# First layer's last four token blocks in two pairs by seven products, and another order of the seven

## The chip, the core and the metric

One core of one Trainium2 chip runs the whole program. The time is device microseconds of one execution; the kernel before takes 1685.62 us (median of three runs, 1683.19 to 1685.78). The engines are named as in the profile: PE (TensorE, matmuls), PEld (its weight loads), DVE (VectorE), ACT (ScalarE), POOL (GpSimd), SP (SyncE, which issues the DMAs).

## What is computed

Linear attention with a normalization, then two layers of a two-matrix network on 4608 tokens of 512 values, the hidden width being 2048:

```python
kv = einsum('bhsd,bhse->bhde', k, v);  out = einsum('bhsd,bhde->bhse', q, kv)   # 8 batches, 8 heads, 576 tokens, 64
x = out / sqrt(mean(out * out, -1) + 1e-06) * g_norm                            # -> [4608, 512]
r = maximum(x @ w_in1, 0);   x = (s * (r * r) + b) @ w_out1                     # first layer
h = x @ w_in2;               y = (h * (1 / (1 + exp(-h)))) @ w_out2             # second layer
```

The weights come as 64-bit floats.

## The kernel before, in words

**Tiles.** Tokens go in nine blocks of 512 (`NB = 9`): block t < 8 holds 512 of batch t's 576 tokens, block 8 the 64 that are left of each. A block of activations is four tiles of 128 x 512. Every fp32 operand of a matmul is split into a rounded part `hi` (written by ACT) and a rest `lo` (a subtraction with two SBUF inputs on DVE or POOL, line 191), and each product takes three matmuls: hi x hi, hi x lo, lo x hi.

**A unit** (`unit`, L611 on) is one block with one 128-wide slice m of the hidden width, m = 0..15: 12 matmuls into a bank `h` (`mm1`), the activation, square and affine on ACT and DVE, the split into `gh` and `gl`, and 12 matmuls that add into four banks `acc` (`mm2`), which come 1.6 units later. The first layer is nine blocks of 16 units. During a block, `attention_pair` (L368 on) makes the next block's activations, two heads at a time, in four steps; `decode` (L219 on) turns the 64-bit weights into fp32; `factors` (L320 on) does so for the second layer's weights, forms the four sums that the seven products want and writes eight quarters of each weight in split form to DRAM.

**Pairs.** In the second layer blocks 0 to 7 go in four pairs by Strassen's seven products, for the hidden product alone. `pair_x` (L760 on) loads half the inner dimension of two blocks (kk = 0 or 1) into the one tile `x32`, forms T1 to T4 (four subtractions of 128 x 512, three of them in the tile `xt`) and splits seven operands into the tiles `xo0..xo6`. `hidden(tp, j)` (L820 on) does two slices of the hidden width at once: seven products of six matmuls in three banks X, Y, Z, in the order X, Y, Z, X, Y, Y, Z. Between two products that share a bank DVE reads the bank (x1, u2, u3, h22): these are partial sums, and the next product adds on top. `outputs(tp, j)` (L919 on) multiplies by the second matrix as before: eight tiles of six matmuls, each added by DVE into a sum `y2` in SBUF (L940). One j is thus 42 + 48 matmuls in place of 48 + 48. The last block goes by units.

**Order.** All instructions are handed to `Plan`, which sorts them by a key (units of the program) and by costs of its own for every engine, and emits each engine's list in a fixed order. At run time each engine goes through its list in that order and waits at whatever is not ready. SBUF space changes hands by name: `lent_to` says which weight tile becomes which `xo`, `win`, `wout` or `g2` tile once the first layer's last block has used it:

```python
        wanted = [f"xo{i}{kk}" for i in range(7) for kk in range(KH)] + ["win"] * 6 + ["wout"] * 5 + ["g2"] * 7
                lent_to[f"w{kind}{m}"] = wanted[2 * m + (kind == "o")]
```

## Time and profile before

| | |
|---|---|
| median of 3 runs | 1685.62 us (1683.19 to 1685.78) |
| the profiled execution | 1683.55 us, its span 1681.2 us |
| PE busy | 1642.5 us (98%), 7744 matmuls |
| DVE, ACT, POOL busy | 51%, 39%, 34% |
| chain that ended last | PE 91% |
| mean granted TensorE clock | 0.991 |

How to read it: busy times are shares of an engine's own time and say nothing of who waits. Matmuls overlap in the records (one lasts some 390 ns, but the next begins long before it ends), so the rate of PE is read from how many start in a stretch, or from the chain of waits, not from the mean of one. A stretch of the windows view gives busy time and instructions of each engine, the granted clock, the share of the DMA engines and GB/s. In time the program is: 0 to 80 us start and block 0, blocks 1 to 8 by units up to 906 us, four pairs up to 1575 us, the last block up to 1662 us, the last store.

### The profile page before, as it was taken

The page shows a single profiled execution, that of the slowest core. Times are in us where ns is not written, and L with a number is a line of the kernel's source. Part 1 is how long each engine was busy: PE and PEld are TensorE (multiplying, and loading weights), DVE is VectorE, ACT ScalarE, POOL GpSimd, SP SyncE. Part 2 cuts the span into 40 slices and gives each one's busy share as a digit, 9 for nine tenths or more (in the row PEclk, how much of TensorE's full clock was granted, in tenths as well). Part 3 has the DMA queues.
Part 4 walks back from the last instruction along what each step waited for, and adds up shares of the span by engine and source line. Part 5 has one row for each costly group of instructions (what it writes and reads, how often), then busy time and mean ns, then how long its engine had stood idle before and what let it go on. Part 6 is the DMA issues. An engine that isn't in the chain of part 4 may idle for free.

```text
span 1681.2 us, 21306 instructions
## 1 busy us (share of the span) xinstructions
PE 1642.5 (98%) x7744; PEld 1334.1 (79%) x7744; DVE 865.4 (51%) x1313; ACT 658.5 (39%) x1198; POOL 565.3 (34%) x481
## 2 busy tenths in 40 slices
PE   8889999999999999999999999999999999999995
PEld 6667888888888888888887888888888888888884
DVE  6998666675656666534342244634463445344211
ACT  5666444444444444432333322432343234323221
POOL 4665343333434344210341223622362235223100
PEclk9989999999999999999999999999999999999998
DMA  9554445444444544210134444644464447444552
GB/s 218 173 157 125 134 127 158 139 147 126 138 143 129 168 122 150 99 63 1 51 116 128 126 145 140 229 156 143 142 232 148 139 138 237 138 140 141 183 156 81
DMA packets 226911, 236.28 MB, mean 141 GB/s; under 512 B 99832, under 2 KB 181752, under 8 KB 226680
## 3 DMA queue, kind: packets, MB, share of 16 engines
q1 hardware_dynamic: 226680, 234.94, 45.4%
q8 instruction: 61, 1.00, 0.3%
q14 instruction: 42, 0.34, 0.1%
q0 software_dynamic: 128, 0.00, 0.0%
HBM read 181.41 MB, written 53.48 MB: 140 GB/s over the span
## 4 chain that ended last, share of the span: by engine, by line
PE 91%; DVE 3%; DMA 1%; ACT 1%; issue 1%; SPq 1%; POOL 0%; DVEq 0%; ACTq 0%; POOLq 0%
PE hp L836 18%; PE h L184 8%; PE h L185 8%; PE h L183 8%; PE acc L183 8%; PE acc L184 7%; PE acc L185 7%; PE acc L931 7%; PE acc L932 7%; PE acc L930 7%; PE kv_ps L433 1%; PE acc L687 1%; PE acc L686 1%; PE acc L685 1%; DVE raw L263 1%
## 5 line engine op out<-in xcount | busy, mean ns | idle before, releaser
L836 PE MATMUL hp<-xo,win 128*128 128x512 f32 x1344 | 344.0, 390 | 0.8 <-DVE tmp L861 0.8
L191 POOL TENSOR_TENSOR g<-tmp,g 128x512 fp32r<-128x512 f32 x123 | 159.3, 1296 | 425.0 <-ACT g L188 223.5
L836 PEld LDWEIGHTS hp<-xo,win 128*128 128x128 f32 x1344 | 252.0, 188 | 57.6 <-DVE tmp L861 2.2
L940 DVE TENSOR_TENSOR y<-acc,y 128x512 f32<-128x512 f32 x224 | 154.3, 690 | 275.1 <-PE acc L932 273.0
L183 PE MATMUL acc<-gh,wo 128*128 128x512 f32 x576 | 234.4, 407 | 2.9 <-ACT gh L188 2.9
L184 PE MATMUL acc<-gl,wo 128*128 128x512 f32 x576 | 226.9, 394 | 5.8 <-DVE gl L191 2.8
L629 ACT ACTIVATE g<-h 128x512 f32<-128x512 f32 x160 | 95.5, 597 | 346.8 <-PE h L185 337.6
L184 PE MATMUL h<-xl,wi 128*128 128x512 f32 x576 | 226.8, 394 | 1.7 <-DVE xl L191 1.6
L183 PE MATMUL h<-xh,wi 128*128 128x512 f32 x576 | 226.5, 393 | 0.1
L185 PE MATMUL h<-xh,wi 128*128 128x512 f32 x576 | 226.1, 393 | 0.3 <-DVE wi L191 0.3
L185 PE MATMUL acc<-gh,wo 128*128 128x512 f32 x576 | 226.1, 392 | 0.0
L637 DVE SCALAR_TENSOR_TENSOR g<-g,vecs 128x512 f32<-128x512 f32 x128 | 104.0, 813 | 197.1 <-ACT g L629 197.0
L932 PE MATMUL acc<-wout,g 128*128 128x512 f32 x512 | 201.7, 394 | 0.0
L931 PE MATMUL acc<-wout,g 128*128 128x512 f32 x512 | 201.7, 394 | 0.0
L930 PE MATMUL acc<-wout,g 128*128 128x512 f32 x512 | 201.3, 393 | 0.0
L861 DVE TENSOR_TENSOR tmp<-hp,tmp 128x512 f32<-128x512 f32 x160 | 110.4, 691 | 99.3 <-PE hp L836 93.9
L665 DVE SCALAR_TENSOR_TENSOR gl<-g,vecs,gh 128x512 fp32r<-128x512 f32 x128 | 112.4, 878 | 49.3 <-ACT gh L659 48.1
L282 POOL TENSOR_TENSOR dw<-raw 128x256 uint32<-128x256 uint32 (+1 forms) x100 | 88.8, 890 | 137.3 <-DVE raw L268 87.3
L184 PEld LDWEIGHTS acc<-gl,wo 128*128 128x128 f32 x576 | 108.9, 189 | 28.1 <-DVE gl L191 4.4
L191 POOL TENSOR_TENSOR spill<-dw,spill 128x512 fp32r<-128x512 f32 x53 | 71.5, 1350 | 176.5 <-ACT spill L188 171.2
L184 PEld LDWEIGHTS h<-xl,wi 128*128 128x128 f32 x576 | 109.0, 189 | 27.2 <-DVE xl L191 3.7
L183 PEld LDWEIGHTS acc<-gh,wo 128*128 128x128 f32 x576 | 109.0, 189 | 26.4 <-ACT gh L188 4.2
(123 smaller groups left out, 2303.1 us busy)
## 6 DMA issues: line engine op xcount, KB each, us to landing
win<-wi SPq DMA_DIRECT2D x96, 512.0 KB, 4.5
wout<-wo SPq DMA_DIRECT2D x160, 256.0 KB, 4.1
wi<-spill SPq DMA_DIRECT2D x32, 512.0 KB, 2.6
wo<-spill SPq DMA_DIRECT2D x32, 512.0 KB, 2.9
win<-wi SPq DMA_DIRECT2D x64, 256.0 KB, 3.2
raw<-in_moe_w_out_dram SPq DMA_DIRECT2D x38, 256.0 KB, 3.0
y<-y SPq DMA_DIRECT2D x36, 256.0 KB, 2.6
raw<-in_moe_w_in_dram SPq DMA_DIRECT2D x34, 256.0 KB, 2.8
```

What stands on the lines that cost most here:

```text
L183: nc.tensor.matmul(ps, wh, xh, start=first, stop=False)
L184: nc.tensor.matmul(ps, wh, xl, start=False, stop=False)
L185: nc.tensor.matmul(ps, wl, xh, start=False, stop=last)
L191: eng[e].tensor_tensor(lo, src, f32(hi), op=ALU.subtract)
L637: nc.vector.scalar_tensor_tensor(out=g_t[u], in0=g_t[u], scalar=s_t, in1=g_t[u], op0=ALU.mult, op1=ALU.mult)
L665: nc.vector.scalar_tensor_tensor(out=st["g"][1], in0=g_t[u], scalar=b_t, in1=f32(st["g"][0]), op0=ALU.add, op1=ALU.subtract)
L836: nc.tensor.matmul(ps, w[:, wn, f_], x_[:, xn], start=first and n == 0, stop=kk == KH - 1 and n == 2, skip_group_check=True)
L861: nc.vector.tensor_tensor(t, bank[me, a], tmp[b_, me], op=ALU.add)
L930: nc.tensor.matmul(ps, g[:, 0, dd], w[:, 0], start=f == 0, stop=False)
L931: nc.tensor.matmul(ps, g[:, 0, dd], w[:, 1], start=False, stop=False)
L932: nc.tensor.matmul(ps, g[:, 1, dd], w[:, 0], start=False, stop=f == 1)
L940: nc.vector.tensor_tensor(y2[tp, tt], st["ps"], y2[tp, tt], op=ALU.add)
```

## The change

**First layer.** Five blocks (`NPL = 5`) go by units; blocks 5 and 6, and 7 and 8, go in two pairs by the same seven products as in the second layer; six pairs in all (`PAIRS`), the second layer's four behind them.

- The activations of blocks 5 to 8 are written to DRAM (`x1_d`) and loaded again by `pair_x`. Attention for blocks 2 to 6 is put into the first five blocks, more densely (a table of keys), for block 7 into the first pair, and block 8 (`last_block`) behind it.
- `factors_first` forms the four sums of the first layer's `w_in` for each j, splits them and writes them to DRAM, with the three plain quarters that are multiplied and all 16 tiles of `w_out`, since these tiles are lent out after block 4 and not after block 8. In each j: two additions of 128 x 512, four of 128 x 256, two roundings and two rests of 128 x 512 (ACT; DVE or POOL), and nine DMAs on SP.
- `xt` loses its place in the pool `l2p` and becomes tile `wi12`, lent after block 4's slice 12; `win` has 5 places in the first layer's pairs (6 before), and 7 later; the tiles `g`, `gh`, `gl` and `y` are handed on as `tmp`.
- In the first layer's pairs each of the four hidden tiles of a j takes a square and an affine step beside the activation (ACT, DVE or POOL); bank Y is one of the four `acc` banks, since attention has `at`.
- `factors` for the second layer's 16 sets is spread over keys 6.4 apart (6 before), and so runs into the first pair.

**Both layers.** The seven products are made in the order X, Y, Z, Y, X, Y, Z: the two products on Y that followed one another directly now have one on X between them. `T4` takes the place of B21 in `x32`.

The core of the diff:

```diff
@@ constants and buffers
-    NPR = (NB - 1) // 2
+    NPL = 5
+    PAIRS = [(0, t) for t in range(NPL, NB, 2)] + [(1, t) for t in range(0, NB - 1, 2)]
+    NPR = len(PAIRS)
...
-    A11, S2, S1, A12, S3, A22, S4, A21 = range(8)
+    A11, S2, S1, S3, A12, A22, S4, A21 = range(8)
@@ def factors_first(j, key), new
+        for f in range(2):
+            add(both(DM), key + 0.1 * f, total(f), needs=[("late",), ("mm1o", KF + 2 * j, 0)] + whole("i", 2 * j + f) + [("fw", 0) + me] * f,
+                makes=[("fw", f) + me], takes=[("dw2", me)] * (f == 0), gives=w_lent("i", 2 * j + f))
+        for o, a, b_, op in ((4, 2, 3, ALU.add), (6, 0, 2, ALU.subtract), (5, 4, 0, ALU.subtract), (7, 1, 5, ALU.subtract)):
...
+            add(both(QW), key + 0.3 + 0.02 * o, go, needs=[("fw", 1) + me] + ([("sum", o - 1 if o == 5 else 5) + me] if o in (5, 7) else []),
+                makes=[("sum", o) + me])
...
+            add(act(2 * QW), key + 0.7 + 0.1 * g, hi, needs=sums, makes=[("fh", g) + me], takes=[sp])
+            add(both(2 * QW), key + 0.72 + 0.1 * g, lo, needs=[("fh", g) + me], makes=[("fl", g) + me], gives=[("dw2", me)])
@@ normalize
+        if paired:
+            add({"SP": 0.48}, key + 0.9, lambda e: dma(x1_d[t, :, p], st["xa"]), needs=[("x32", t, p)], makes=[("xd", t, p)],
+                gives=[xb], move=0.73)
@@ units
-    units = {(l * NB + t) * KF + m: (l, t, m) for l in range(2) for t in range(NB) for m in range(KF) if l == 0 or t == NB - 1}
+    units = {(l * NB + t) * KF + m: (l, t, m) for l in range(2) for t in range(NB) for m in range(KF) if t == NB - 1 or t < NPL
+             if (t < NPL) == (l == 0)}
@@ pairs
-    B11, T2, T1, B21, T3, T4, B22 = range(7)
+    B11, T2, T1, T3, B21, T4, B22 = range(7)
-    BANK = (X, Y, Z, X, Y, Y, Z)
+    BANK = (X, Y, Z, Y, X, Y, Z)
@@ pair_x
-                dma(t[:, 2 * h:2 * h + 2], y1[2 * tp:2 * tp + 2, :, kk + KH * h].rearrange("n p t -> p n t"))
+                dma(t[:, 2 * h:2 * h + 2], (x1_d, y1)[layer][n0:n0 + 2, :, kk + KH * h].rearrange("n p t -> p n t"))
-                    st["t"] = pools["l2p"].tile([P, 3, T], F32, tag="xt", name="xt")
+                    st["t"] = f32(place(("xt", me)))
@@ hidden
+        ybank = "at" if layer else "acc"
-        read = {3: "x1", 4: "u2", 5: "u3", 6: "h22"}
+        read = {3: "u2", 4: "x1", 5: "u3", 6: "h22"}
...
+            if layer == 0:
+                add({**act(T), **both(T)}, kk + 0.03, squares, needs=[last], makes=[("sq2",) + q_])
+                add({**act(T), DVE: 0.46}, kk + 0.06, affine, needs=[("sq2",) + q_], makes=[("sa",) + q_])
@@ program
-                factors(kind, j, KF + 3 + 6 * (2 * j + n))
+                factors(kind, j, KF + 3 + 6.4 * (2 * j + n))
+            factors_first(j, 20 + 6 * j)
-        wanted = [f"xo{i}{kk}" for i in range(7) for kk in range(KH)] + ["win"] * 6 + ["wout"] * 5 + ["g2"] * 7
+        wanted = [f"xo{i}{kk}" for i in range(7) for kk in range(KH)] + ["win"] * 5 + ["wout"] * 5 + ["xt"] + ["g2"] * 7
+        more = {"tmp": 4, "g2": 3, "win": 2}
-                    attention_pair(t, p, KF * (t - 1) + (0.5 + 3.2 * p if t > 1 else 0.75 + 3.4 * p))
-                split_x(t, p, KF * t - 0.8)
+                    k0, dk = {1: (0.75, 3.4), 2: (16.5, 3), 3: (32.5, 2.8), 4: (48.5, 2.2), 5: (57, 2.2), 6: (65, 2.2), 7: (80, 3)}[t]
+                    attention_pair(t, p, k0 + dk * p)
+                if t < NPL:
+                    split_x(t, p, KF * t - 0.8)
-        last_block(KF * (NB - 2) + 6)
+        last_block(94)
```

**What moves in the engines' lists.** The lists of all engines are the same as before up to block 1's first unit (on PE the first 824 rows, on DVE the first 198; the program's lines have other numbers in the changed kernel: L183 to L185 are L186 to L188, L191 is L194, L836 is L922, L861 is L947, L940 is L1050). In the names, `_49` and the like in brackets are semaphores of the engine or DMA lane that is waited for.

First place: PE, where the units end and the first pair begins, from the first product's kk = 0 on. Before (block 8 to the second layer's first pair):

```order
L836 MATMUL hp_8240<-xo00_7693,win_7923 128x512 [waits DMAHW6_49]
L836 MATMUL hp_8240<-xo00_7693,win_7923 128x512 [waits Pool_49]
L836 MATMUL hp_8240<-xo00_7693,win_7923 128x512
L183 MATMUL acc_7712<-gh_8216,wo14_1662 128x512
L184 MATMUL acc_7712<-gl_8217,wo14_1662 128x512
L185 MATMUL acc_7712<-gh_8216,wo14_1662 128x512
L836 MATMUL hp_8240<-xo01_7956,win_7923 128x512
L836 MATMUL hp_8240<-xo01_7956,win_7923 128x512 [waits Pool_49]
L836 MATMUL hp_8240<-xo01_7956,win_7923 128x512
```

Now (block 4 to the first layer's first pair), and on to slice 15:

```order
L922 MATMUL hp_5595<-xo00_5415,win_5105 128x512 x2
L186 MATMUL acc_4704<-gh_5527,wo14_1687 128x512
L187 MATMUL acc_4704<-gh_5528,wo14_1687 128x512
L188 MATMUL acc_4704<-gh_5527,wo14_1687 128x512
L922 MATMUL hp_5595<-xo01_5549,win_5105 128x512 [waits Activation_49]
L922 MATMUL hp_5595<-xo01_5549,win_5105 128x512 [waits DVE_49]
L922 MATMUL hp_5595<-xo01_5549,win_5105 128x512
L186 MATMUL acc_4741<-gh_5527,wo14_1687 128x512
L187 MATMUL acc_4741<-gh_5528,wo14_1687 128x512
L188 MATMUL acc_4741<-gh_5527,wo14_1687 128x512
L186 MATMUL acc_4672<-gh_5601,wo15_1755 128x512 [waits Activation_49]
L187 MATMUL acc_4672<-gh_5602,wo15_1755 128x512 [waits DVE_49]
```

The same turn has moved from behind block 8 to behind block 4, with the same products between; `xo01`, the operand of kk = 1, now comes from DVE and not from POOL.

Second place: DVE at that same turn. Before, the rows ahead of the first read of bank Y (L861):

```order
L637 SCALAR_TENSOR_TENSOR g_8174<-g_8174,vecs_103 128x512 [waits Activation_49]
L665 SCALAR_TENSOR_TENSOR gl_8185<-g_8174,vecs_103,gh_8184 128x512 [waits PE_49,Activation_49]
L637 SCALAR_TENSOR_TENSOR g_8206<-g_8206,vecs_103 128x512 [waits Activation_49]
L665 SCALAR_TENSOR_TENSOR gl_8217<-g_8206,vecs_103,gh_8216 128x512 [waits PE_49,Activation_49]
L637 SCALAR_TENSOR_TENSOR g_8238<-g_8238,vecs_103 128x512 [waits Activation_49]
L665 SCALAR_TENSOR_TENSOR gl_8249<-g_8238,vecs_103,gh_8248 128x512 [waits PE_49,Activation_49]
L861 TENSOR_TENSOR tmp_8279<-hp_8260,tmp_8258 128x512 [waits PE_49,Activation_49]
```

Now, the rows between the split of slice 14 and that of slice 15 (the gl of before is called gh too):

```order
L283 TENSOR_SCALAR raw_5510<-raw_5510 128x256 [waits DMAHW6_49,Pool_49]
L268 TENSOR_SCALAR raw_5510<-raw_5510 128x256 [waits Activation_49]
L862 TENSOR_TENSOR x32_5492<-x32_5492 128x512 [waits DMAHW5_49,DMAHW4_49,Pool_49]
L273 SCALAR_TENSOR_TENSOR raw_5510<-dw_5478,raw_5510 128x256 [waits DVE_49]
L283 TENSOR_SCALAR raw_5517<-raw_5517 128x256 [waits DMAHW7_49]
L268 TENSOR_SCALAR raw_5517<-raw_5517 128x256 [waits Activation_49]
L194 TENSOR_TENSOR xo01_5549<-x32_5492,xo01_5549 128x512
L273 SCALAR_TENSOR_TENSOR raw_5517<-dw_5478,raw_5517 128x256 [waits DVE_49]
L717 SCALAR_TENSOR_TENSOR g_5560<-g_5560,vecs_128 128x512 [waits Activation_49]
L194 TENSOR_TENSOR xo21_5579<-xt_5537,xo21_5579 128x512 [waits Activation_49]
L194 TENSOR_TENSOR xo31_5591<-x32_5492,xo31_5591 128x512 [waits Activation_49]
L745 SCALAR_TENSOR_TENSOR gh_5602<-g_5560,vecs_128,gh_5601 128x512 [waits PE_49,Activation_49]
```

Before, nothing but the units' own rows stood here; now the decode of the second layer's weights and the making of kk = 1's operands stand between them. Behind them follow three sums of `factors` and a `raw` row, kvl of block 7's attention, a y copy, a spill rest, a transpose, a `raw` row, `xo51` and a reduction, and then the first read of Y.

Third place: DVE in the middle of a pair. Before, a stretch that repeats from j to j in the second layer:

```order
L861 TENSOR_TENSOR tmp_8901<-hp_8820,tmp_8824 128x512 [waits PE_49,Pool_49]
L861 TENSOR_TENSOR tmp_8901<-hp_8851,tmp_8901 128x512 [waits DVE_49]
L940 TENSOR_TENSOR y2_8453<-acc_8894,y2_8453 128x512 [waits PE_49]
L940 TENSOR_TENSOR y2_8469<-acc_8909,y2_8469 128x512 [waits PE_49]
L861 TENSOR_TENSOR tmp_8928<-hp_8820,tmp_8824 128x512 [waits PE_49,Pool_49]
L940 TENSOR_TENSOR y2_8491<-acc_8930,y2_8491 128x512 [waits PE_49]
L861 TENSOR_TENSOR tmp_8849<-hp_8851,tmp_8849 128x512 [waits PE_49]
```

Now, in the first layer's first pair, between two reads of a bank:

```order
L947 TENSOR_TENSOR tmp_6557<-hp_6559,tmp_6557 128x512 [waits PE_49]
L1050 TENSOR_TENSOR y2_6070<-acc_6696,y2_6070 128x512 [waits PE_49]
L592 RECIPROCAL rms_6721<-rms_6721 128x16 [waits Activation_49]
L596 STREAM_TRANSPOSE inv_6734<-rms_6721 128x512 [waits DVE_49]
L613 SCALAR_TENSOR_TENSOR kv_6650<-kv_6650,vecs_128,inv_6734 128x512 [waits DMAHW1_49,DMAHW0_49,DVE_49]
L283 TENSOR_SCALAR raw_6703<-raw_6703 128x256 [waits DMAHW5_49,Pool_49]
L980 TENSOR_SCALAR tmp_6557<-tmp_6557,vecs_128 128x512 [waits Pool_49]
L268 TENSOR_SCALAR raw_6703<-raw_6703 128x256 [waits Activation_49]
L283 TENSOR_SCALAR raw_6709<-raw_6709 128x256 [waits DMAHW6_49]
L273 SCALAR_TENSOR_TENSOR raw_6703<-dw_6662,raw_6703 128x256 [waits DVE_49]
L268 TENSOR_SCALAR raw_6709<-raw_6709 128x256 [waits Activation_49]
L1050 TENSOR_TENSOR y2_5882<-acc_6736,y2_5882 128x512 [waits PE_49]
```

What in the second layer is a list of reads of banks is here mixed with attention, decode and the affine step. Counted from the first read of Y in j = 0 to that in j = 4, DVE's list has 111 rows, and from there to that in j = 8, which is the second pair's first, 129; in the second layer of the kernel before such stretches have 41 and 65 rows.

## Rows read from the trace of the kernel before

**Rows 1.** The page's part 1: busy us, share, instructions by engine.

```profile
PE 1642.5 (98%) x7744; PEld 1334.1 (79%) x7744; DVE 865.4 (51%) x1313; ACT 658.5 (39%) x1198; POOL 565.3 (34%) x481
```

**Rows 2.** Windows: stretch, length, busy PE PEld DVE ACT POOL (count), clock, DMA, GB/s.

```profile
40.00:80.00 40.00, 33.24 (x153) 25.12 (x152) 39.69 (x50) 26.17 (x50) 24.14 (x19) 0.96 0.59 180
240.00:280.00 40.00, 40.00 (x209) 32.34 (x208) 25.61 (x40) 18.55 (x36) 18.16 (x17) 1.00 0.47 151
880.00:920.00 40.00, 39.22 (x172) 31.82 (x171) 12.20 (x15) 12.79 (x20) 4.96 (x4) 1.00 0.42 134
1120.00:1160.00 40.00, 40.00 (x175) 32.63 (x175) 17.10 (x26) 10.58 (x17) 9.70 (x8) 1.00 0.45 140
...
920.00:1575.00 655.00, 655.00 (x2849) 534.53 (x2848) 283.57 (x405) 224.01 (x365) 221.85 (x169) 1.00 0.51 161
```

**Rows 3.** The chain, six matmuls within a pair: start, us, what.

```profile
930.38 1.36 PE hp L836 x6
```

**Rows 4.** Groups by form, PE, the pairs' hidden product.

```profile
L836 PE MATMUL hp<-xo,win 128*128 128x512 f32 x1344 | 344.0, 390 | 0.8 <-DVE tmp L861 0.8
```

**Rows 5.** Groups by form: count, busy us, mean ns of one, idle before.

```profile
L861 DVE TENSOR_TENSOR tmp<-hp,tmp 128x512 f32<-128x512 f32 x160 | 110.4, 691 | 99.3 <-PE hp L836 93.9 <-POOL g L191 0.7
L637 DVE SCALAR_TENSOR_TENSOR g<-g,vecs 128x512 f32<-128x512 f32 x128 | 104.0, 813 | 197.1 <-ACT g L629 197.0
L665 DVE SCALAR_TENSOR_TENSOR gl<-g,vecs,gh 128x512 fp32r<-128x512 f32 x128 | 112.4, 878 | 49.3 <-ACT gh L659 48.1
L268 DVE SCALAR_TENSOR_TENSOR raw<-dw,raw 128x256 uint32<-128x256 uint32 x72 | 35.3, 494 | 1.7
L263 DVE TENSOR_SCALAR raw<-raw 128x256 uint32<-128x256 uint32 x72 | 23.1, 323 | 12.4 <-ACT dw L259 11.3
L278 DVE TENSOR_SCALAR raw<-raw 128x256 uint32<-128x256 uint32 x64 | 39.5, 624 | 11.0 <-DMA raw<-in_moe_w_in_dram 5.5 <-DMA raw<-in_moe_w_out_dram 5.3
L338 DVE TENSOR_TENSOR dw<-dw 128x256 f32<-128x256 f32 x15 | 10.0, 668 | 0.0
L191 DVE TENSOR_TENSOR spill<-dw,spill 128x512 fp32r<-128x512 f32 x11 | 13.8, 1252 | 6.6 <-ACT spill L188 6.5
L191 DVE TENSOR_TENSOR g<-tmp,g 128x512 fp32r<-128x512 f32 x5 | 7.6, 1529 | 3.6 <-ACT g L188 3.6
L191 DVE TENSOR_TENSOR xo<-xt,xo 128x512 fp32r<-128x512 f32 x13 | 15.6, 1221 | 0.0
L191 DVE TENSOR_TENSOR xo<-x,xo 128x512 fp32r<-128x512 f32 x7 | 4.8, 679 | 0.0
L781 DVE TENSOR_TENSOR x<-x 128x512 f32<-128x512 f32 x8 | 8.7, 1088 | 2.0 <-DMA x<-y 1.5 <-POOL xt L781 0.5
L781 POOL TENSOR_TENSOR xt<-x,xt 128x512 f32<-128x512 f32 x16 | 25.3, 1580 | 2.7 <-DMA x<-y 1.6
L191 POOL TENSOR_TENSOR xo<-x,xo 128x512 fp32r<-128x512 f32 x29 | 40.2, 1392 | 27.9 <-ACT xo L188 27.6
L191 POOL TENSOR_TENSOR g<-tmp,g 128x512 fp32r<-128x512 f32 x123 | 159.3, 1296 | 425.0 <-ACT g L188 223.5 <-PE acc L932 195.1 <-issue 6.1
```

**Rows 6.** Timeline, DVE and POOL, operands of a pair: start, us, what.

```profile
869.49 1.78 DVE L191 TENSOR_TENSOR xo<-xt,xo 128x512 fp32r<-128x512 f32 x1
874.59 0.68 DVE L191 TENSOR_TENSOR xo<-x,xo 128x512 fp32r<-128x512 f32 x1
...
868.98 5.14 POOL L191 TENSOR_TENSOR xo<-x,xo 128x512 fp32r<-128x512 f32 x3
```

**Rows 7.** Windows of 4 us in block 0, columns as in rows 2.

```profile
56.00:60.00 4.00, 2.00 (x8) 1.08 (x7) 4.00 (x6) 1.31 (x3) 1.91 (x2) 1.00 0.91 274
60.00:64.00 4.00, 3.92 (x11) 3.11 (x12) 4.00 (x8) 3.91 (x8) 2.49 (x2) 0.63 0.37 139
```

**Rows 8.** DMA issues of pair loads (KB, us to landing); a window of 10 us.

```profile
x<-y SPq DMA_DIRECT2D x16, 512.0 KB, 5.2
...
1400.00:1410.00 10.00, 10.00 (x45) 8.18 (x44) 7.84 (x9) 4.72 (x8) 7.57 (x6) 1.00 0.99 339
```

More of the change, by code (lines that the diff above doesn't have):

```diff
@@ L360, with w_lent @@
+    def w_lent(kind, m):
+        return [(lent_to[f"w{kind}{m}"], f"w{kind}{m}")]
     x_t = {}
@@ L537, in spread @@
             )
+        xb = ("kv", me) if t == NB - 1 else ("sq", me)
+        paired = t >= NPL
+        last = t == NB - 1
         def x(e):
-            if t < NB - 1 and p == 0:
-                new_x(t)
-            nc.vector.scalar_tensor_tensor(
-                out=x_t[t][:, p], in0=src(), scalar=gn, in1=st["inv"], op0=ALU.mult, op1=ALU.mult
-            )
+            if paired:
+                dst = src() if last else st["sq"]
+                st["xa"] = dst
+            else:
+                if p == 0:
+                    new_x(t)
+                dst = x_t[t][:, p]
+            nc.vector.scalar_tensor_tensor(out=dst, in0=src(), scalar=gn, in1=st["inv"], op0=ALU.mult, op1=ALU.mult)
         add(act(T), key, sq, needs=needs, makes=[f("sq")], takes=[("sq", me)])
@@ L577, in place, with small @@
         tag = plan.place[b]
-        return (pools["late"] if tag in [f"w{kd}{m}" for kd, m in late] else wp).tile([P, 2, DM], F32R, tag=tag, name=b[0])
+        pool = pools["l2p"] if tag[0] == "e" else pools["late"] if tag in [f"w{kd}{m}" for kd, m in late] else wp
+        return pool.tile([P, 2, DM], F32R, tag=tag, name=b[0])
+    def small(b, n=None, dtype=F32):
+        tag = plan.place[b] if n is None else plan.place[b][n]
+        return (pools["l2p"] if tag[0] == "e" else tp).tile([P, T], dtype, tag=tag, name=b[0])
     def split_x(lb, kk, key):
@@ L627, in first @@
         def first(e):
-            g_t[u] = tp.tile([P, T], F32, tag="g", name="g")
+            g_t[u] = small(g)
             nc.scalar.activation(g_t[u], h_t[u], AF.Relu if layer == 0 else AF.Silu)
@@ L717, in out_y @@
             if not final:
-                st["y"] = tp.tile([P, T], F32, tag="y", name="y", bufs=2)
+                st["y"] = small(yb)
             else:
@@ L762, in pair_x @@
         me = (tp, kk)
+        layer, n0 = PAIRS[tp]
         xb = ("x32", ("pair",) + me)
@@ L851, in new @@
         def new(n):
-            t = tmp[n, me] = pools["l2p"].tile([P, T], F32, tag="tmp", name="tmp", bufs=plan.room["tmp"])
+            t = tmp[n, me] = small(tb[n])
             return t
@@ L874, in hidden, with squares, affine @@
         add({DVE: 0.69}, k(6), plus("a", Z, "a"), needs=done(6) + [("h22",) + me], makes=[("h12",) + me], gives=[bk[Z]])
-        for f, n, src, ready, kk in ((0, 0, "d", done(3) + [("x1",) + me], k(3)), (1, 1, "b", [("h22",) + me], k(4) + 0.1),
+        for f, n, src, ready, kk in ((0, 0, "d", done(4) + [("x1",) + me], k(4)), (1, 1, "b", [("h22",) + me], k(3) + 0.1),
                                      (1, 0, "c", [("h21",) + me], k(5) + 0.1), (0, 1, "a", [("h12",) + me], k(6) + 0.1)):
             def silu(e, src=src):
-                if src == "d":
-                    nc.scalar.activation(new("d"), bank[me, X], AF.Silu)
-                else:
-                    nc.scalar.activation(tmp[src, me], tmp[src, me], AF.Silu)
+                from_ = bank[me, X] if src == "d" else tmp[src, me]
+                nc.scalar.activation(new("d") if src == "d" else from_, from_, AF.Silu if layer else AF.Relu)
+            def squares(e, src=src):
+                t = tmp[src, me]
+                if e == ACT:
+                    nc.scalar.activation(t, t, AF.Square)
+                else:
+                    eng[e].tensor_tensor(t, t, t, op=ALU.mult)
+            def affine(e, src=src):
+                t = tmp[src, me]
+                if e == ACT:
+                    nc.scalar.activation(t, t, AF.Identity, scale=s_t, bias=b_t)
+                else:
+                    nc.vector.tensor_scalar(t, t, s_t, b_t, op0=ALU.mult, op1=ALU.add)
             gb = ("g2", me + (f, n))
@@ L916, in outputs @@
         me = (tp, j)
+        layer, n0 = PAIRS[tp]
         for n in range(2):
@@ L951, in store @@
                     def store(e, tt=tt, n=n, d=d):
-                        r = (2 * tp + n) * S + d * P
-                        dma(out[r:r + P, :], y2[tp, tt])
-                    add({"SP": 0.48}, key + 0.6, store, needs=[("yt", tp, j, tt)], makes=[("out", tp, tt)], gives=[yb], move=0.73)
+                        r = (n0 + n) * S + d * P
+                        dma(out[r:r + P, :] if layer else y1[n0 + n, :, d], y2[tp, tt])
+                    add({"SP": 0.48}, key + 0.6, store, needs=[("yt", tp, j, tt)], makes=[("out", tp, tt) if layer else ("y", n0 + n, d)],
+                        gives=[yb], move=0.73)
     with tc.manual_schedule():
```

158 lines of the change are left out of this document (115 added, 43 removed).

## The prediction, made before the changed kernel ran

> **What bounds the kernel now.** Read first the page's part 1: PE is busy 98% of the span [rows 1], while no other engine reaches 52%. Then the windows, since a share of the whole says nothing of a stage: behind block 0 PE is busy all 40 us of a stretch, and only the one with the turn to the pairs lacks 0.78 us [rows 2]. So from 160 us on this kernel is a row of matmuls without a gap, and fewer of them is time saved, if nothing else comes up to PE. Third, what one matmul costs. The groups give a mean of 390 ns [rows 4], but records overlap: the chain has six in 1.36 us [rows 3], and the 40 us window at 1120 us holds some 176 records, full [rows 2]. Both give 0.227 us. That is the price to use; with 390 ns the saving would come out 1.7 times too large.
>
> Last, which engine is next. In the blocks DVE is busy 25.6 of 40 us, in the pairs 283.6 of 655 [rows 2]. At 40 to 80 us it shows what a full DVE does: 39.7 us busy, and PE at 33.2 of 40 [rows 2]. That stage isn't touched (the lists are the same up to there), but it is the likeness by which I judge the new ones.
>
> **The change, part by part.** *Matmuls.* Two pairs of 8 j, each j with 42 in place of 48: 96 fewer, times 0.227 us: **21.8 us** less. Attention's matmuls move but stay as many.
>
> *Order of the seven.* PE waited for a bank's reader 0.8 us in all, once, at the old turn [rows 4]. More than that the new order cannot give; 0.8 us goes with the old turn, and nothing else in the second layer is charged or credited: its pairs have no wait to lose.
>
> *The turn behind block 4.* This is new where before there was slack. Set zero where slice 12's `mm1` ends: only then is `wi12` free, the new place of `xt`, so only then can DVE form T1. Then come, each behind the other, T1 on DVE 1.1 us, T2 and T4 on POOL at 1.6, two `lo` between them on POOL at 1.4 [rows 5], and the last rest on DVE at 1.2: 8.3 us, with waits between engines and units' rows among them some 10. Then `x32` is free and kk = 1's load goes out, 5.2 us to landing [rows 8], the raw tile whose decode stands first on DVE behind it: 17. DVE now has seven rows up to `xo01`: 0.62, 0.32, 1.09, 0.49, 0.62, 0.32, 0.68 = 4.1 us [rows 5]; `xo01` is there at about 21. PE has three units (72 matmuls) and 12 more before it wants `xo01`, and a small attention step: 84 x 0.227 = 19.1, say 19.7. It waits 1.5 us. Next it has five matmuls (1.1 us) while DVE does 0.49, 0.81, 1.22, 0.68 and 0.88 up to slice 15's `gl`: 4.1; 3.0 us of waiting. Then three sums of 0.67 and a raw row of 0.62 up to `kvl` against seven matmuls: 1.0. Then y (0.69, as L861), a spill rest 1.25, a raw row 0.62, `xo51` 0.68, two rows taken at 0.7 and the first read of Y 0.69: 5.3 against 19 matmuls (4.3): 1.0. Sum 6.5 us. Where PE idled two of four us in block 0, the next four were granted 0.63 of the clock, that is most of them at 1.2 and not at 2.4 GHz [rows 7], a loss of 4 x 0.37 = 1.5. I take **8 us**. Bounds: 0.8, as at the old turn; 16, if the DVE rows take what they take beside a busy POOL (below).
>
> *The first pair of the first layer.* DVE has 111 rows up to the fifth j's first read of Y and 129 up to the ninth's. A row costs 25.61/40 = 0.64 us in the blocks, 39.69/50 = 0.79 at 40 to 80 us, and 283.57/405 = 0.70 in the pairs [rows 2]. I take 0.70, since reads of banks and additions (0.69 each [rows 5]) are the largest part, as there: 78 and 90 us. PE in the second of these has 4 x 42 matmuls and 36 outputs of six, for 36 of the rows are additions to `y2`: 384 x 0.227 = 87.2 us. In the first it has 4 x 42 and 25 outputs, 318 x 0.227 = 72.2, and block 7's attention, about 6 by its dozen split matmuls and its small ones: 78. So DVE is even with PE in the first half and 3 us behind in the second. An engine this full can't make up a wait in order, so I add 4 (an estimate; there is no row for it): **7 us**. Bounds: 0 at 0.64; at 0.79, 10 in the first and 15 in the second, 25.
>
> *The rest.* Blocks 1 to 4 get 89 to 120 DVE rows each, at 0.64 some 57 to 77 us of 87; `factors_first` lies mostly on POOL, which is under half busy there [rows 2]. The second pair has 86 and 99 rows, 60 and 69 us. Covered, but in a fixed order; **1 us** for all, between 0 and 4. The ACT work added (squares, affine, rounding at some 0.6 us) hides under an engine that is 39% busy [rows 1]. SP has 183 rows more; its DMAs are priced in a rival. If DVE's cover goes, all of these show up as waits of PE for `gl`.
>
> *Sum.* 1683.55 - 21.8 - 0.8 + 8 + 7 + 1 = 1676.95 for an execution like the profiled one; the median of the runs lies 2.07 above that one: **1679.0 us**, 6.6 less than before. By the bounds alone the case spans 1664 to 1708; with 4 to 12 us for the turn and 3 to 11 for the pair, as I hold likely, 1671 to 1687.
>
> **Rivals.** *All of it is hidden.* The turn costs what the old one did, DVE keeps 0.64 a row: 1685.6 - 21.8 = 1664. For it: all that DVE gets is at most even with PE. Against: the chain at the turn is fixed by the `wi12` tile, and 17 us of it are no matter of DVE's speed.
>
> *DVE stretched by POOL: slower.* Beside three POOL instructions in 5.14 us a DVE rest took 1.78 us, and 0.68 when POOL was quiet [rows 6]. In the first pair 35 rows of 512 are of this kind, with both inputs in SBUF (13 rests of the hidden tiles, 7 of spills, 7 of operands, 3 subtractions, 2 squares, 3 normalizations). In the rows priced above they stand at some 1.2 on average; at 1.78 they cost 20 us more, and longer waits of PE bring the lower clock behind them (1.5 each, up to 8 of them in eight j). Half of these 32: 1679 + 16 = 1695, range 1687 to 1706. It decides if DVE's mean row in the pair passes 0.74 (10 us more over 240 rows). For it: at 40 to 80 us POOL was busy 24 of 40 and DVE's row was 0.79. Against: in the pairs, with POOL at a third, 0.70.
>
> The Trainium skill (SBUF — State Buffer, section SBUF: two separate sides) goes further: the port pair that VectorE and GpSimd share is an exclusive lock, held for a whole instruction, and the loser is fully blocked. By that rule each of the 35 rows would wait out up to a whole POOL instruction, and the time would be about 1706. The trace doesn't bear it out whole: three POOL rows took 1.71 us each and the DVE rows beside them 1.78, at the same time, where alone they take 1.30 and 0.68 [rows 5, 6]; one behind the other would be 1.98.
>
> *DMA becomes the bound.* From the first pair's first `win` load to its fifth j's SP issues 28.1 MB by the shapes in its list, to the second pair's first another 22.5, for 78 and 87 us: 360 and 260 GB/s. The pairs before moved 140 at a share of 0.45 (311 at a full one); at a share of 0.99 it was 339 [rows 2, 8]. So the first half may run 5 to 12 us late, in place of DVE's loss or on top: 1684. Against: weights are loaded four tiles ahead, 20 us of PE's time, and the loads of the first j start before the turn.
>
> That the change doesn't do what it says is excluded for the matmuls, which are 96 fewer in PE's list; for the other order of the seven it holds nearly, as there was only 0.8 us to win.
>
> **How the numbers follow.** A measurement of this kernel can tell about 0.2% (3.4 us) from no change, so faster is below 1682.2 and slower above 1689.0. Chances: the forecast 0.50 (0.42 of it faster, 0.07 same, 0.01 slower), all hidden 0.18 (faster), DVE stretched 0.22 (0.02 same, 0.20 slower), DMA 0.10 (0.10 same or a little to either side: 0.02 faster, 0.07 same, 0.01 slower). Together faster 0.62, same 0.16, slower 0.22. The range goes from the hidden case, 1664, to the middle of the stretched one, 1696, and leaves out the upper half of that, about 0.1, and a little below.
>
> **What would show it.** In the profile after: 96 matmuls fewer, at the same 0.227 us; PE full from 160 us to the turn at about 600; there waits of PE for `xo01` from DVE, `gl` and the first Y read, 5 to 10 us in two or three pieces, and a clock below 1; in the pair behind it DVE at 9 tenths or more and waits of PE for L947 and the rests of `g2`, some us each half; from the second pair on no waits. The second layer's pairs as long as before, 164 us each. Wrong would be: PE waits in the turn under 2 us or over 16; DVE's row in the first pair under 0.65 or over 0.74; waits for `win` or `wout` loads above all others; or time lost in blocks 3 and 4, whose units I take as covered.

## The result, and the profile after

The changed kernel takes 1693.39 us (median of 5 runs, 1690.89 to 1697.23), the kernel before 1685.25 beside it: a ratio of 1.0060, 95% interval 1.0048 to 1.0071. It is **slower by 0.6%**, where 0.4% faster was forecast. The profiled execution spans 1691.0 us, 9.8 more than that of before.

The page's part 1 of the changed kernel, against [rows 1] (busy us, share, instructions):

```profile
PE 1628.2 (96%) x7648; PEld 1314.1 (78%) x7648; DVE 978.0 (58%) x1474; ACT 727.9 (43%) x1337; POOL 678.3 (40%) x573
```

PE is busy 14.3 us less and idle 24.1 us more. The place shows in the windows, columns as in [rows 2]: the turn behind block 4, the first layer's two pairs, and for comparison a stretch of the second layer from another answer of the same view.

```profile
530.00:572.00 42.00, 35.39 (x155) 26.85 (x154) 34.26 (x43) 20.14 (x39) 24.50 (x18) 0.92 0.54 188
572.00:736.00 164.00, 159.81 (x744) 127.95 (x743) 126.64 (x219) 94.73 (x175) 78.48 (x71) 1.00 0.74 245
736.00:910.00 174.00, 168.46 (x723) 134.95 (x722) 126.38 (x196) 97.05 (x167) 89.50 (x80) 1.00 0.71 238
...
960.00:1200.00 240.00, 240.00 (x1050) 196.83 (x1049) 109.67 (x156) 75.17 (x125) 76.35 (x58) 1.00 0.49 156
```

The second layer is a row of matmuls without a gap, as before. In the first layer's pairs PE has gaps, though VectorE is busy only 126.64 of 164 us (77%) and 126.38 of 174 (73%), and its mean row there is 126.64/219 = 0.58 us. No engine is full.

To size the gaps I took the starts of all PE records in order, and counted as lost what lies between two starts beyond 0.2273 us, for each 128x512 matmul. Both profiled executions then add up: 6815 such matmuls before and 6719 after, 96 fewer, -21.8 us; lost 48.2 before and 78.9 after, +30.6; small matmuls of the attention +0.9. Sum +9.7 of the 9.8. By stage (us lost; a stage ends where the first product of the next one starts, so block 4 ends at 556.0 us and the rest of its turn counts to the first pair; for before, the units of blocks 4 to 8 stand in place of block 4 and the two pairs; the runs of the other rows follow below):

```
                    blocks 0-2   3   block 4   pair 1   pair 2   second layer
before                    30.8  1.9   ------ 6.6 ------            8.9
changed                   31.6  3.3     9.0     17.5      9.7      7.8
a1_old_order              30.9  3.3    10.5     23.7     14.2      8.3
a5_dve_prep               30.8  3.3     7.9     15.3      8.0      5.9
b1_slack                  31.4  3.3     9.4     10.1      8.5     10.4
b2_slack_prep             30.5  3.3     3.4     10.1      7.8     10.2
d1_wide                   31.1  3.3     3.0     10.2     10.2     10.1
e1_some_copies            31.4  3.3    11.6     25.4     13.3      8.8
e2_less_loads             31.9  3.3     8.4     22.7     11.1      8.4
```

What PE waited for from 440 to 910 us, where the kernel before has no such row from 440 to 906 (waits of PE: us in total, times, longest):

```profile
PE acc L187 <- DVE gh L745: 4.9, 3, 2.6
PE hp L922 <- DVE xo L194: 3.8, 2, 2.6
PE m_ps L585 <- DVE part L578: 3.6, 5, 1.0
PE acc L187 <- POOL g L194: 1.7, 2, 0.9
PE o_ps L188 <- DVE kvl L194: 1.0, 1, 1.0
...
PE kv_ps L494 <- ACT orem L198: 0.7, 1, 0.7
```

Many short waits: for the rests of block 4's last hidden tiles (`gh`, L745) at the turn, the next pair's operands (`xo`) at the turn between the pairs, and one step of the attention after another. None is for a load. In the records they are 20 waits, and by the starts they carry 23.0 of the 36.7 us lost from 440 to 910; 2.5 more go with a lower clock at the turn (below), and the other 11.2 have no waiting row of their own (the kernel before lost 6.7 from 440 to 906, without one wait).

One thing grew more than any engine's work, the transfers (windows of before and of the changed kernel, the last two columns):

```profile
440.00:906.00 466.00, 466.00 (x2256) 381.61 (x2255) 248.17 (x388) 183.91 (x344) 144.04 (x128) 1.00 0.34 108
440.00:910.00 470.00, 450.75 (x2083) 359.60 (x2082) 348.59 (x557) 254.07 (x469) 226.44 (x199) 0.99 0.71 230
```

The turn, as PE's timeline shows it (start, us, what, idle before and its releaser), and the granted clock behind it in windows:

```profile
558.57 0.40 PE L188 MATMUL acc<-gh,wo 128*128 128x512 f32 x1
559.76 0.50 PE L186 MATMUL acc<-gh,wo 128*128 128x512 f32 x1 [0.79 <-ACT gh L739]
562.84 0.50 PE L187 MATMUL acc<-gh,wo 128*128 128x512 f32 x1 [2.57 <-DVE gh L745]
...
564.83 0.63 PE L187 MATMUL o_ps<-qTl,kvh 128*128 128x512 f32 x1
566.41 0.80 PE L188 MATMUL o_ps<-qTh,kvl 128*128 128x512 f32 x1 [0.96 <-DVE kvl L194]
...
568.37 0.63 PE L186 MATMUL acc<-gh,wo 128*128 128x512 f32 x1
568.80 0.63 PE L187 MATMUL acc<-gh,wo 128*128 128x512 f32 x1
```

```profile
557.00:564.00 7.00, 3.64 (x16) 2.48 (x15) 7.00 (x6) 2.67 (x6) 6.48 (x6) 1.00 0.55 159
564.00:571.00 7.00, 6.04 (x16) 4.09 (x15) 5.64 (x11) 2.86 (x6) 2.62 (x2) 0.52 0.39 140
571.00:575.00 4.00, 4.00 (x19) 3.29 (x18) 1.05 (x2) 1.81 (x3) 1.29 (x1) 0.99 0.88 218
```

Behind 3.4 us of waiting (0.79 + 2.57) the next 7 us had 0.52 of the clock, almost all at 1.2 GHz and not at 2.4: matmuls start 0.43 us apart.

Why `gh` is late shows at the turn's first wait, in PE's timeline (the matmul behind that of 539.67 could have started 0.23 us after it, at 539.9), VectorE's and GpSimd's:

```profile
539.67 0.39 PE L186 MATMUL acc<-gh,wo 128*128 128x512 f32 x1
542.03 0.50 PE L187 MATMUL acc<-gh,wo 128*128 128x512 f32 x1 [1.97 <-DVE gh L745]
```


```profile
534.43 1.80 DVE L862 TENSOR_TENSOR xt<-x 128x512 f32<-128x512 f32 x1 [2.51 <-PE h L188]
536.15 0.74 DVE L717 SCALAR_TENSOR_TENSOR g<-g,vecs 128x512 f32<-128x512 f32 x1
536.81 1.78 DVE L862 TENSOR_TENSOR x<-x 128x512 f32<-128x512 f32 x1
538.52 1.78 DVE L194 TENSOR_TENSOR xo<-x,xo 128x512 fp32r<-128x512 f32 x1
540.22 1.75 DVE L745 SCALAR_TENSOR_TENSOR gh<-g,vecs,gh 128x512 fp32r<-128x512 f32 x1
```

```profile
536.31 1.74 POOL L862 TENSOR_TENSOR xt<-x,xt 128x512 f32<-128x512 f32 x1 [0.63 <-DVE xt L862]
538.01 1.74 POOL L194 TENSOR_TENSOR xo<-xt,xo 128x512 fp32r<-128x512 f32 x1
539.71 1.71 POOL L194 TENSOR_TENSOR xo<-x,xo 128x512 fp32r<-128x512 f32 x1
```

VectorE first stands 2.5 us, with the `xt` row at the head of its queue, until slice 12's `mm1` lets the tile go. Then operand rows, whose first product PE starts only at 556.0, go ahead of the `gh` that PE wants now, each at 1.78 us beside GpSimd.

### The profile page after: what moved, and what is told of

The parts are those of the page before. It is cut to its first block, busy times and chain, and to the rows that moved or that the text cites. A ratio compares the mean times of both kernels' runs of the same rounds, so it can differ in the third digit from the quotient of the medians.

```text
span 1691.0 us, 21854 instructions
## 1 busy us (share of the span) xinstructions
PE 1628.2 (96%) x7648; PEld 1314.1 (78%) x7648; DVE 978.0 (58%) x1474; ACT 727.9 (43%) x1337; POOL 678.3 (40%) x573
## 5 line engine op out<-in xcount | busy, mean ns | idle before, releaser
L922 PE MATMUL hp<-xo,win 128*128 128x512 f32 x2016 | 521.9, 392 | 5.9 <-DVE xo L194 4.9
L922 PEld LDWEIGHTS hp<-xo,win 128*128 128x128 f32 x2016 | 377.9, 188 | 91.7 <-DVE xo L194 6.6
L1050 DVE TENSOR_TENSOR y<-acc,y 128x512 f32<-128x512 f32 x336 | 230.3, 687 | 297.8 <-PE acc L1042 268.6
L194 POOL TENSOR_TENSOR g<-tmp,g 128x512 fp32r<-128x512 f32 x155 | 202.5, 1313 | 438.5 <-ACT g L191 327.4
L966 ACT ACTIVATE tmp<-tmp 128x512 f32<-128x512 f32 x144 | 90.6, 629 | 337.2 <-DVE tmp L947 337.1
L947 DVE TENSOR_TENSOR tmp<-hp,tmp 128x512 f32<-128x512 f32 x240 | 165.2, 688 | 86.6 <-PE hp L922 82.0
L194 POOL TENSOR_TENSOR spill<-dw,spill 128x512 fp32r<-128x512 f32 x59 | 78.8, 1336 | 163.0 <-ACT spill L191 153.2
L187 PE MATMUL acc<-gh,wo 128*128 128x512 f32 x320 | 127.3, 398 | 12.8 <-DVE gh L194 5.9
L186 PE MATMUL acc<-gh,wo 128*128 128x512 f32 x320 | 132.7, 415 | 4.9 <-ACT gh L191 3.6
L187 PE MATMUL h<-xl,wi 128*128 128x512 f32 x320 | 125.4, 392 | 1.3 <-DVE xl L194 1.2
L186 PE MATMUL h<-xh,wi 128*128 128x512 f32 x320 | 125.7, 393 | 0.5 <-ACT xh L191 0.5
L188 PE MATMUL acc<-gh,wo 128*128 128x512 f32 x320 | 126.0, 394 | 0.0
L191 ACT ACTIVATE g<-tmp 128x512 fp32r<-128x512 f32 x192 | 119.9, 629 | 12.7 <-DVE tmp L980 7.0
L188 PE MATMUL h<-xh,wi 128*128 128x512 f32 x320 | 125.1, 391 | 0.3 <-DVE wi L194 0.3
L1042 PEld LDWEIGHTS acc<-wout,g 128*128 128x128 f32 x512 | 96.1, 188 | 21.7
L1041 PEld LDWEIGHTS acc<-wout,g 128*128 128x128 f32 x512 | 96.1, 188 | 21.1
L1040 PEld LDWEIGHTS acc<-wout,g 128*128 128x128 f32 x512 | 96.2, 188 | 20.8
```

The costliest lines, as they stand in the source:

```text
L186: nc.tensor.matmul(ps, wh, xh, start=first, stop=False)
L187: nc.tensor.matmul(ps, wh, xl, start=False, stop=False)
L188: nc.tensor.matmul(ps, wl, xh, start=False, stop=last)
L191: nc.scalar.activation(hi, src, AF.Copy)
L194: eng[e].tensor_tensor(lo, src, f32(hi), op=ALU.subtract)
L922: nc.tensor.matmul(ps, w[:, wn, f_], x_[:, xn], start=first and n == 0, stop=kk == KH - 1 and n == 2, skip_group_check=True)
```

## The experiments

Theory, from this profile: **order**. PE, VectorE and the others go through rows in an order written beforehand by `Plan`, from costs that the chip doesn't keep (0.61 us for a VectorE rest that took 1.78). Where a result is later than the plan has it PE has a hole, though the engines have room. Rivals: **load** (VectorE and GpSimd are too full there, my prediction's mechanism) and **transfers** (their share was 0.7). Ratios are to runs of the kernel before on the same chip; the changed kernel's own is 1.0060.

**One part of the change alone.** r1_order_alone: the kernel before with these lines of the change and the reads that belong to them.

```
-    B11, T2, T1, B21, T3, T4, B22 = range(7)
-    BANK = (X, Y, Z, X, Y, Y, Z)
+    B11, T2, T1, T3, B21, T4, B22 = range(7)
+    BANK = (X, Y, Z, Y, X, Y, Z)
```

> The kernel before with one part of the change alone: the new order of the seven products in its second layer. In the changed kernel the row of matmuls loses 4.3 us between 930 and 1575 us against 0.227 us per matmul, in the kernel before 7.7 us between 930 and 1562. Theory that the order gives this: 3.4 us less than before, 1682. Rival, that it comes from the new places of tiles and not from the order: the time before, 1685, within 1 us. My prediction said 0 to 0.8 us.

1682.63 us, ratio 0.9993 (0.9984 to 1.0002): at most 2.7 us, with no change possible. a1_old_order takes the same lines back in the changed kernel.

> The changed kernel with the old order of the seven products in both layers. If the order is worth 3.4 us in the second layer and as much per j in the first layer's 16 j, it is 3 to 5 us slower than the changed kernel: 1697 to 1699. If the order is worth nothing: 1693, within 1 us.

1708.25 us, 1.0147 (1.0132 to 1.0161): 15 us slower than the changed kernel, a miss for both expectations. The second layer loses 8.3 us, nearly as with the new order, and the first layer's pairs 23.7 + 14.2. PE's waits there:

```profile
PE hp L922 <- DVE tmp L947: 7.7, 9, 2.3
PE m_ps L585 <- DVE part L578: 6.2, 6, 1.9
```

The first was 0.3 us in all with the new order. So two products on one bank side by side cost nothing that can be told in the kernel before and much here, where VectorE's reads come late. These waits are half of the 15 us; the other half lies at other waits of a list that the edit rewrote.

**Less work.** a3_no_square_affine: `if layer == 0:` ahead of the two rows in `hidden` made false.

> The changed kernel without the squares and the scale-and-shift of the hidden tiles of the first layer's two pairs (this part of the computation is left out; 128 instructions less on ACT, DVE and POOL, some 90 us of engine time in 365 us). Load theory (VectorE and GpSimd are too full from block 3 to the end of the second pair, and PE's waits follow the load): at least half of the 22 us that PE loses from 572 to 930 us come back, 1682 or less. Order theory (each wait is one place where the written order asks for a result a little too early, on engines with room): only the waits for the tiles g2 go, 3 to 5 us, and the turn, the attention's waits and the turns between pairs stay: 1688 to 1690.

1688.51 us, 1.0033 (1.0020 to 1.0047): some 4.5 us less than the changed kernel, what the order theory gives, and under half of the 11 us that the load theory wants for 90 us of engine time.

**VectorE and GpSimd side by side.** a5_dve_prep: `both(T)` to `dve(T)` in the two places of `pair_x`.

> The changed kernel with the operand differences and the rests of the operand tiles of every pair on VectorE alone, none on GpSimd. At the turn behind block 4 three such instructions of VectorE took 1.78 us each beside three of GpSimd at 1.74. Theory that the two engines side by side are what makes the last unit's rests late: alone six take 6 x 0.68 = 4.1 us in place of 5.3, PE's waits at the turn fall from 7.8 to 4 us and at the turn between the pairs from 5 to 3: 1687. Rival, that VectorE's queue is the limit and each more row in it is a wait: 1697 or more.

1688.87 us, 1.0031 (1.0020 to 1.0042): 4.9 us less, with 73 rows fewer on GpSimd and 75 more on VectorE in the profile. VectorE was busy 357.79 of the 466 us from 440 to 906, for 348.59 of 470, and the kernel was faster, so VectorE's load is not the cause. Most of its operand rows now took 0.68 us. That this is what gave the 4.9 us is likely but not shown: the edit also rewrote the order, and GpSimd, at 188.23 us for 226.44, had less to do.

**The order alone.** b1_slack: in `Plan.run`

```
-                end += self.LAG.get(e, 0.0)
+                end += self.LAG.get(e, 0.0) + (0.4 if 62 <= op[0] < 112 else 0.0)
```

> The changed kernel with 0.4 us more from each instruction's end to the start of what waits for it, in the plan that writes the order, for everything with a key from 62 to 112 (blocks 3 and 4 and the first layer's pairs). Nothing is added or removed on the engines but a few small places in their orders. Order theory (the plan asks for results earlier than the chip has them, on engines with room): the attention's waits (6 us between 440 and 730) and part of the turn's go, 6 to 12 us: 1681 to 1687. Load theory: the same work on the same engines, 1693 within 2 us.

1686.83 us, 1.0015 (1.0006 to 1.0025): 7.6 us less by the ratios. Nothing is left out; results are only asked for later. (The forecast describes the range of keys wrongly: block 4 is 64 to 80, the first pair 80 to 112, and the second pair, 112 to 144, was not covered.) The first pair lost 10.1 us in place of 17.5, the others as before. b2_slack_prep has both edits.

> Two edits that helped alone, together: 0.4 us more of distance in the plan (6.7 us) and the operands' differences and rests on VectorE alone (4.9 us). If they cure different waits (the attention's and those of the g2 tiles; the turns), the sum holds: 1681 to 1683. If both cure the same ones: 1686 to 1688.

1682.37 us, 0.9988 (0.9978 to 0.9997): 12.1 us less, and the two alone make 12.5. So they cure different waits for the most part, as forecast, and block 4 with the start of its turn falls from 9.0 to 3.4, where either alone leaves it at 9.4 and 7.9. c1_costs instead multiplies VectorE's and GpSimd's costs in `add` by 1.3.

> The changed kernel with the costs of VectorE's and GpSimd's instructions taken 1.3 times as long in the plan that writes the order, for keys from 62 to 116 (block 3 to the end of the first layer's pairs); the work is the same. At the turn those two engines took 1.75 to 1.8 us where the plan has 0.61 and 1.22. If the lateness of single results against the written order is the cause, the last units' rests come before the operands' rows or PE's rows behind both: 6 to 10 us less than the changed kernel, 1683 to 1687. If the engines are simply full there, 1692 or more.

1689.90 us, 1.0042 (1.0028 to 1.0057): 3.0 us less, a small gain between the two forecasts; c4_all puts 1.25, 0.3 us and the operands on VectorE together.

> All three together over keys 62 to 116: costs of VectorE and GpSimd 1.25 times as long, 0.3 us more of distance, operands' rows on VectorE alone. Order theory: the turn, the attention's waits and the turns between pairs lose half of their 30 us: 1676 to 1681, faster than the kernel before. Load theory: not under 1686.

1690.02 us, 1.0038 (1.0024 to 1.0052): a miss. Its profiled execution, 1693.71 us, loses 16.0 us in each of the two pairs; stretched costs and distance do not add.

**The late tile.** b3_xt_early: `"xt"` first in `wanted`.

> The changed kernel with the operand differences of a pair in the tile of the weights freed first (slice 0's) in place of slice 12's; every operand tile stands one weight tile later. My prediction built the turn behind block 4 on that tile being late (17 us from its release to the second load's first use). If that is the cause, the differences are made eight units earlier, between rows with room, and 6 to 8 of the 10.6 us lost between 530 and 572 go: 1685 to 1687. If the loss comes from the number of rows that VectorE and GpSimd have in blocks 3 and 4, it only moves: 1691 to 1694.

1694.16 us, 1.0061 (1.0046 to 1.0076): no change. The chain starts 9 us earlier and not eight units: T1 is made at 525.34 in place of 534.43, now behind its load, and that of kk = 1 at 543.62 in place of 551.42. PE's waits for `gh` at the turn are shorter (1.31 and 1.56 in place of 1.97 and 2.57), but others take their place (2.04 for a read of a bank at 569.84); the tile alone is not what the turn hangs on.

**One pair.** b6_one_pair: `NPL = 7`, attention and factors spread.

> The changed kernel with one pair in the first layer (its last two blocks) in place of two: seven blocks by units, the attention and the weights' factors spread over them. 48 matmuls fewer than the kernel before, 10.9 us. If the loss comes from attention and factors squeezed into less time, the turn and the one pair lose some 8 us together and the second layer gives 2 back: 1684 - 10.9 + 8 - 2 = 1679. If every such pair and its turn cost what they cost now (10 at the turn, 10 in a pair), it gains nothing: 1684 to 1691.

1694.09 us, 1.0061 (1.0046 to 1.0076): a miss for both. With half of the matmuls saved it is as slow: the pair and its turns lose 14.2 us, blocks 5 and 6 5.3 and 6.5. So squeezing two pairs into the first layer is not the cause by itself; every new order of this stage that ran had holes.

**Transfers.** b5_twice: each `win` load of layer 0 written twice.

> The changed kernel with every load of the first layer's first weights for a pair issued twice into the same tile (29.4 MB more, some 84 GB/s on top of 235 from 540 to 900 us). If transfers bound the first layer's pairs, as one of the rivals of the prediction had it, 10 us slower or more: 1703 and up. If they are hidden: within 3 us of the changed kernel, 1690 to 1696.

1863.70 us, 1.1064 (1.1046 to 1.1082), 170 us more, most of it not by volume: the same bytes in c3_copies (below) cost 47. SyncE's queue, in which a load into the same tile waits for the first (queue's waits, as above):

```profile
SPq L203 <- DMA win<-wi: 320.0, 67, 8.7
```

c3_copies moves the same bytes with no such wait, e1_some_copies two sevenths (`and g == 0`), e3_copies_second as much as e1 in the second layer (`if tp in (3, 4) and g == 0`, from `w_d[1]`). In b5 and in these three the order of the other four engines is that of the changed kernel, row for row. The edit of c3:

```
+                if not layer:
+                    dma(spare_d[tp * NS + j][:, 2 * g:2 * g + w], w_d[0, "i", j][:, 2 * g:2 * g + w])
```

> The changed kernel with as many bytes more as in the run that loaded the first weights twice (29.4 MB), but copied from one place in memory to another that nothing reads, so that no load waits for another into the same tile. If the transfers' volume bound the first layer's pairs, 20 us slower or more, as there. If that run's 170 us came from SyncE's queue standing behind two loads of one tile (it waited 320 us in 67 waits for the tile's first load), this one is within 10 us of the changed kernel: 1692 to 1703.

> The changed kernel with two sevenths of the added copies (8.4 MB, some 24 GB/s on top of 235). If each byte moved in the first layer's pairs costs from the first one on, 47 us x 2/7 = 13: 1706. If there is room in the transfers and only the full dose ran out of it: within 3 us of the changed kernel, 1691 to 1697.

> The changed kernel with the same 8.4 MB of copies as e1_some_copies, but in the second and third pair of the second layer, where the transfers' share was 0.5 and no attention and no factors run. If a copy costs by its place in SyncE's queue, some 14 us as there: 1707. If it costs only where the other engines' queues stand behind transfers: within 2 us of the changed kernel, 1691 to 1695.

c3: 1740.46 us, 1.0334 (1.0318 to 1.0351). e1: 1707.99, 1.0145 (1.0132 to 1.0158). e3: 1695.03, 1.0061 (1.0046 to 1.0076). So 29.4 MB cost 47 us and 8.4 MB 14.6, 1.6 to 1.7 us per MB, in the first layer's pairs, and nothing that can be told in the second layer. c3 and e1 came out as the rival of transfers had it. Then the other way, e2_less_loads: `w = 2 if g < 3 and layer else 1`, and `i % 2 if layer else 0` in `mm`.

> The changed kernel with 12.6 MB less to load in the first layer's pairs: of each two sevenths of the first weights only one is loaded and used for both products (the other's weights are left out of the computation; the matmuls, and all work on the other engines, are the same). Transfer theory (between blocks 3 and the end of the first layer ScalarE and VectorE stand for transfers, and what is queued behind them comes late): at 1.6 us per MB as in the two runs with more, 20 us less, of which 10 to 20 can be had from some 30 lost: 1673 to 1683. Order theory alone: 1693 within 2 us.

1699.40 us, 1.0091 (1.0074 to 1.0108): a miss, 6 us slower with 12.6 MB less. What ScalarE waited for from 440 to 920 us, first in the changed kernel (the two largest rows), then here:

```profile
ACT spill L191 <- DMA wi<-spill: 21.3, 8, 5.7
ACT spill L191 <- DMA wo<-spill: 16.6, 9, 6.1
```

```profile
ACT spill L191 <- DMA wi<-spill: 14.3, 8, 2.8
ACT spill L191 <- DMA wo<-spill: 12.3, 6, 4.4
```

ScalarE stood less for transfers, and PE lost more. The plan knew of the smaller loads and wrote another order (by the traces some 55 rows moved on PE and 150 on VectorE), which outweighed it. Transfers that come late against a given order cost time; that their volume bounds this stage is not borne out. How much of the 30.6 us they carry stays open: no run had fewer bytes under the same order. It may be much, since the kernel before moved 108 GB/s here and the changed one 230, and the same two waits of ScalarE were short before:

```profile
ACT spill L188 <- DMA wo<-spill: 6.6, 5, 2.9
ACT spill L188 <- DMA wi<-spill: 3.8, 4, 1.4
```

e2 is also a warning for the runs above. Every edit of the changed kernel but b5 and the copies rewrites the order, and here a rewriting cost 6 us or more by itself; so a3, a5 and c1, each worth 3 to 5 us, decide little alone.

**To the end.** d1_wide and d2_wide6: b2_slack_prep with 0.4 and 0.6 us over keys 46 to 150; d4_factors: d1_wide with 5.4 in place of 6.4 in the key of `factors`.

> The changed kernel with 0.4 us more of distance in the plan for keys from 46 to 150 (the stretch in b1_slack ended with the first pair, so its second pair and the turn behind it kept their waits: 7.8 and 6.9 us) and the operands' rows on VectorE alone. Order theory: the second pair and its turn lose 4 to 8 us less: 1674 to 1679. Rival, that these two wait for full engines or transfers: 1681 to 1683, as without the wider stretch.

> As d1_wide with 0.6 us in place of 0.4. If single lateness of that size is what is left: 1 to 3 us less than d1_wide. If the distance now pushes work itself later (buffers are held longer): slower than d1_wide by 1 to 5 us.

> As d1_wide, with the second layer's factors every 5.4 slices in place of 6.4, so that they end some 15 slices earlier (about the end of the first pair's first half) and lie more in blocks 1 to 4. Load theory: the first layer's pairs lose 5 us or more less, blocks 3 and 4 no more than 2 us more: 1672 to 1676. Order theory: no change against d1_wide within 2 us.

d1_wide: 1680.59 us, 0.9984 (0.9975 to 0.9993). d2_wide6: 1691.40, 1.0045 (1.0032 to 1.0058). d4_factors: 1681.63, 0.9986 (0.9977 to 0.9994). d1_wide beats both kernels, by 2.7 us and by 12.8, but is no better than b2_slack_prep within the intervals: the two pairs still lose 10.2 us each, so what is left there isn't cured by this distance. 0.6 us is worse, by 10.8 us where 1 to 5 were expected. Earlier factors change nothing, as the order theory has it.

## Why the prediction was wrong

- **Matmuls**: right, 96 fewer, 21.8 us.
- **Old turn and second layer**, -0.8: about right, 7.8 us lost for 8.9. The new order alone is worth nothing sure in the kernel before (r1_order_alone); its worth of 15 us lies in the first layer's pairs (a1_old_order), which I had not looked at.
- **Turn**, 8 us: 11.2 lost from 530 to 572 us, against some 0.9 before: 10.3. The size was near, in part by luck: PE waited for `gh` and `kvl` and had half a clock, as listed, but for `xo01` and the read of Y it did not wait, and 2.3 us for the `gh` of earlier slices (up to 542.03 and 548.09) were not in the list. The 17 us from `wi12`'s release were not the cause (b3_xt_early). What stood ahead of the late `gh` were rows out of turn, slowed beside GpSimd; b2_slack_prep, which changes both, bears that out, and neither edit alone does.
- **First pair**, 7 us: 9.4 lost from 572 to 736, against some 3.2: 6.2. The size held by luck, and the reason fell. VectorE's row took 0.58 us, not 0.70, and it was busy at 77%, not 9 tenths; the prediction named a row under 0.65 as a sign against itself.
- **The rest**, 1 us, is **the step that failed**. I wrote of the second pair and blocks 1 to 4 "Covered, but in a fixed order" and took busy time for the cover; time lost in blocks 3 and 4 was a sign against the prediction by its own words. Lost there: 0.8 in blocks 0 to 2, 1.4 in block 3, 4.2 in block 4 ahead of the turn, 8.8 in the second pair with the turn into it; together 15.2 us. That is nearly the whole miss: 14.2 more than the term, and 1679.0 + 14.2 is 1693.2. The errors of the other terms (2.3 too little for the turn, 0.8 too much for the first pair, and smaller ones) nearly cancel.
- **The rival that VectorE is stretched by GpSimd** gave 1695, near the time, by a price of 1.78 us a row that is right where operands are made (1.78, 1.78, 1.75 above, as [rows 6]). But its point of decision, a mean row over 0.74, did not come, and of VectorE's 23 operand rows from 440 to 910 us only 7 took over 1.5 us; their mean was 1.17, near the 1.2 that the sum already held. a5_dve_prep, which takes the operands off GpSimd, gave 4.9 us, not 16. The Trainium skill's exclusive lock (SBUF — State Buffer, section SBUF: two separate sides) is again not borne out whole: at the turn the rows of either engine start 1.70 us apart (VectorE's 536.81, 538.52, 540.22; GpSimd's 536.31, 538.01, 539.71), where one behind the other makes 0.68 + 1.30 = 1.98. It is not far: side by side saves 14%, and VectorE alone does two such rows in 1.36.
- **The rival of transfers** asked for waits of PE for `win` or `wout` loads; PE had none. At one remove it isn't excluded: ScalarE's two waits for transfers rose from 10.4 to 37.9 us, and more bytes under the same order cost PE time at once (e1_some_copies).

The miss in short: 30.6 us more were lost, most of them at waits for late results in stages taken as covered. More written distance and the operands on VectorE alone take back 12 together (b2_slack_prep); that the same work in another order is worth 7.6 of them is shown (b1_slack), though not that the distance as such gives it, since 0.6 us was worse than 0.4; that the rest is due to the two engines side by side (a5_dve_prep) is argued. What is left, about 10 us in the first pair and 8 in the second at best, stayed in every order in the table. Its cause is open, and transfers that come late are the rival that no run settles.

## What to carry to other kernels

Where a list of costs writes the order, "busy 75%, so covered" does not hold: ask for each new row which row it is put ahead of, and how late that one may be. A change that rewrites such an order pays for its holes before it earns its matmuls; try more distance between dependent rows in the plan first, in more than one size, and measure an edit on the changed kernel, since an order of products worth nothing in one was worth 15 us in the other.
